# Second mixture: transposing DMAs for the gathered rows and the gate rows, and a fetch of all rows of an expert one expert ahead

## The chip, the cores and the metric

The kernel runs on one core of one Trainium2 chip. The metric is the device time of one execution in microseconds (us). Differences below about 0.2% (4 us) cannot be told from no change.

## What is computed

```python
attn_out = _attn_ref(q, k, v, alpha)                    # gated linear attention: 4 x 8 heads, 768 steps, head size 48
x = attn_out.transpose(0, 2, 1, 3).reshape(B * S, H * D)   # 3072 tokens x 384
x = _moe_ref(x, w_gate, w1, w2)                         # first mixture: all 8 experts on all tokens
# second mixture: the two best of 8 experts for every token
logits = x @ w_gate
noisy_logits = logits + np.log1p(np.exp(x @ w_noise)) * noise
top2 = np.argpartition(-noisy_logits, 2, axis=1)[:, :2]
top2_w = softmax of the two
for e in range(E):
    for k in range(2):
        mask = top2[:, k] == e
        h = np.maximum(x[mask] @ w1[e], 0.0)            # 384 -> 1024
        out[mask] += top2_w[mask, k, None] * (h @ w2[e])   # 1024 -> 384
```

## The kernel before, in words

Attention, the first mixture and the second mixture follow each other on TensorE, and each overlaps the next at its border. Every product is made from float16 high and low parts: three matmuls stand for one.

**Gate rows.** When a tile T of 128 tokens (of 24) is done in the first mixture, `a1` (line 684) makes the high and low float16 halves of its rows, `x` [128, 768], and sends them to DRAM (`xd`, line 688, SP's queue). `a2` (line 691) turns them into columns: six TensorE transposes of 128x128 (line 695) into a PSUM bank, copied to `xf` by ScalarE (line 697). `a3` (line 699) is the gate's matmuls on `xf` (lines 704 and 706). After tile 13 (`G1T` = 14 tiles), and again after tile 23, `route` picks the two best experts of each token and counts ranks.

**Rows of an expert.** An expert has `NJ` = 7 blocks of slots: blocks 0 to 2 (`J0` = 3, 384 slots) and blocks 3 to 6 (448 slots, the last block has 64). `lanes`, `index_rhs` and `index` (lines 802 to 834) make the row numbers of the blocks (a small product, line 815), `gather` (line 839) fetches the 128 rows of a block from `xd` with an indirect DMA of GpSimd's queue into one of eight buffers (`rows`, the room of tiles 0 to 7 of `acc`), and `xpose` (line 847) turns them into columns by six TensorE transposes (line 851) and a ScalarE copy (line 852) into `xh` (even experts) or `xl` (odd experts). In all there are 24 calls of `a2` and 56 of `xpose`.

**Products.** `g1b` (line 854) is the first product of an expert: nine matmuls a unit (line 862), eight units. `g2b` (line 868) is the second: 24 matmuls a block (line 225), a scaling on VectorE (line 874) and an indirect DMA of GpSimd's queue that adds the rows to the output (line 875). The order of stages is (expert 0, blocks 0 to 2), (1, 0 to 2), (0, 3 to 6), (1, 3 to 6), and from expert 2 on both parts of an expert in turn.

**What sets the order.** The program is written in one fixed order. Next to the stream of matmul units a planner's clock runs: after every unit `pump(t)` adds its cost (1.97 for a unit of the first mixture's first product, 0.98 after every pair of `f` steps of a second product, 1.46 for a unit of `g1b` over 384 slots), and `chain` lists of side work have their next item written into the program when the clock has reached its due time; the number beside an item is the time until the next one is due. `need(tag)` pumps without matmuls until a tag is done. `gates` (line 1119) lists a1, a2, a3 for one tile (tiles 0 to 13) or for two (14 to 23), with `GW` = 1.2 after each `a2`. `rows_in` (line 1141) lists lanes, index and gathers, with `GA` = 4.0 after the last gather; `columns` (line 1154) lists the `xpose` calls. `prep` (line 1159) is both. From expert 2 on, at the start of the stage (e, blocks 0 to 2), the chain is `prep(e, J0, NJ)` and then `prep(e + 1, 0, J0)` (line 1242): the late blocks are fetched and turned in the stage before they are used.

**SP's queue.** SP issues the weight loads (lines 111 and 115, two staging buffers `wst`, each load waiting for VectorE's split of the one before the last, line 146), the `xd` stores, and the zeroes written over the output and over `xd` (lines 624 and 628). It works in the program's order, and each entry waits for its own data. GpSimd's queue issues gathers and output additions in the program's order.

Of the kernel before, what the change touches and what calls it, by code (L numbers as in the profile page):

```python
# [10 lines left out]
F16 = mybir.dt.float16  # L11
I32 = mybir.dt.int32
AF = mybir.ActivationFunctionType
# [18 lines left out]

WR = 4.0
GW = 1.2
GA = 4.0
RH = 4.0
SKW = 4.3
# [9 lines left out]
def kernel(ctx, tc, q, k, v, alpha, w_gate, w1a, w2a, g2w, n2w, noise, w1b, w2b, out):  # L47
    nc = tc.nc
    B, NC, _, H, D = v.shape
    E, DM, F = w1a.shape  # L50
    C = 128
    S = NC * C
    NT = B * NC
    NP = H // 2
    KC = DM // 128
# [20 lines left out]
    def bank(shape, dt=F32):  # L76
        return PS["bank"].tile(shape, dt, tag="bank", name="bank")
# [506 lines left out]
    NJ = (H0 + H1 + 127) // 128  # L584
    J0 = H0 // 128
# [4 lines left out]
    G1T = G1  # L590
    BIG = 3.0e38
    OOB = 65536.0
    M2 = {}
# [3 lines left out]
    def m2_setup():  # L597
        sq = ctx.enter_context(tc.tile_pool(name="moe2", bufs=1))
        sr = ctx.enter_context(tc.tile_pool(name="moe2r", bufs=2))
        dr = ctx.enter_context(tc.tile_pool(name="rows", bufs=1, space=bass.MemoryType.DRAM))  # L600
        M2["sr"] = sr
        M2["xd"] = dr.tile([N, 2 * DM], F16, name="xd")

        left_over = [[x, 0] for x in SPARE]

        def t(name, shape, dt=F32):
            n = math.prod(shape[1:]) * (2 if dt == F32 else 1)
            for x in left_over:
                if n >= 384 and x[1] + n <= WT[0].shape[1] - WPL:
                    v = x[0][:, x[1]:x[1] + n]  # L610
                    x[1] += n + n % 2
                    v = v.bitcast(dt) if dt != F16 else v
                    if len(shape) > 2:
                        d = " ".join("abcd"[:len(shape) - 1])
                        v = v.rearrange(f"p ({d}) -> p {d}", **dict(zip("abcd", shape[1:])))
                    M2[name] = v
                    return v
            M2[name] = sq.tile(shape, dt, name=name)
            return M2[name]
# [45 lines left out]
        i16 = t("i16", [128, 128], F16)  # L665
# [16 lines left out]
    XF = {}  # L682

    def a1(T):
        x = M2["sr"].tile([128, 2, DM], F16, name="x16")
        nc.scalar.activation(x[:, 0], acc[:, T, :], AF.Copy, scale=SX2)
        nc.vector.scalar_tensor_tensor(x[:, 1], acc[:, T, :], SX2, x[:, 0], op0=OP.mult, op1=OP.subtract)
        nc.sync.dma_start(M2["xd"][xrow(T):xrow(T) + 128, :], x.rearrange("p a d -> p (a d)"))
        XF[T] = x

    def a2(T):
        x = XF.pop(T)
        p = bank([128, 2 * KC, 128], F16)
        for c in range(2 * KC):
            nc.tensor.transpose(p[:, c, :], x.rearrange("p a (c n) -> p (a c) n", n=128)[:, c, :], M2["i16"])
        XF[T] = M2["sr"].tile([128, 2 * KC, 128], F16, name="xf")
        nc.scalar.activation(XF[T], p, AF.Copy)

    def a3(T):
        x = XF.pop(T)  # L700
        g = M2["g2"]
        p = bank([128, 2, 2 * E])
        for kc in range(KC):
            nc.tensor.matmul(p.rearrange("p a e -> p (a e)"), x[:, kc, :], g[:, kc].rearrange("p a e -> p (a e)"),
                             start=(kc == 0), stop=False, skip_group_check=True)
            nc.tensor.matmul(p[:, 0], x[:, KC + kc, :], g[:, kc, 0], start=False, stop=(kc == KC - 1),
                             skip_group_check=True)
        lo = M2["sr"].tile([128, 2 * E], F32, name="lo")
        nc.scalar.activation(lo, p[:, 1], AF.Copy)
        nc.vector.tensor_add(M2["l2"][:, T, :], p[:, 0], lo)  # L710
# [91 lines left out]
    def lanes(e, T0, T1):  # L802
        for T in range(T0, T1):
            nc.vector.tensor_scalar(M2["lh"][:, T, :], M2["irow"], M2["lane"][:, e, T:T + 1], None, op0=OP.is_equal)

    def index_rhs(e, j0, j1, T1):
        nj = j1 - j0
        nc.vector.tensor_mul(M2["rhs"][:, :T1, j0:j1, :],
                             M2["th"][:, e, :T1, j0:j1, None].to_broadcast([128, T1, nj, 5]),
                             M2["vv"][:, e, :T1, None, :].to_broadcast([128, T1, nj, 5]))  # L810

    def index(e, j0, j1, T1):
        p = bank([128, j1 - j0, 5])
        for T in range(T1):
            nc.tensor.matmul(p, M2["lh"][:, T, :], M2["rhs"][:, T, j0:j1, :], start=(T == 0), stop=(T == T1 - 1))
        slot_rows(p, e, j0, j1)
# [20 lines left out]
    RW = {}  # L837
# [7 lines left out]
        RW[e, j] = r  # L845

    def xpose(e, j, dst):
        r = RW.pop((e, j))
        p = bank([128, 2 * KC, 128], F16)
        for c in range(2 * KC):  # L850
            nc.tensor.transpose(p[:, c, :], r[:, c * 128:(c + 1) * 128], M2["i16"])
        nc.scalar.activation(dst, p[:, :, :dst.shape[2]], AF.Copy)  # L852

    def g1b(x, par, f, xt, n):
        if f == 0:
# [125 lines left out]
    for n, (e, nb) in enumerate(seq):  # L981
        if e == 0 and nb < len(FINE):
            w = FINE[nb]
            a = [[("g1t", 4 * nb + T, w, j) for j in range(FC // 2)] for T in range(0, 4, w)]
# [74 lines left out]
    def chain(items, prio=None):  # L1059
        c = [clk[0], list(items)]  # L1060
        if prio is None:
            chains.append(c)
        else:
            chains.insert(prio, c)
        return c
# [53 lines left out]
    def gates(Ts):  # L1119
        c = []  # L1120
        Ts = list(Ts)
        n = len(Ts)
        for i in range(n + 2):
            if i < n:
                c.append((lambda T=Ts[i]: a1(T), 1.2))
            if 0 <= i - 1 < n:
                c.append((lambda T=Ts[i - 1]: a2(T), GW))
            if i >= 2:
                c.append((lambda T=Ts[i - 2]: a3(T), 0.2, "a3_%d" % Ts[i - 2]))
        return c  # L1130
# [6 lines left out]
    def xt_of(e):  # L1137
        x = xh if e % 2 == 0 else xl
        return x.rearrange("p c n -> p (c n)")[:, :2 * KC * CAP].rearrange("p (c n) -> p c n", n=CAP)

    def rows_in(e, j0, j1, T1, idx_j1):
        c = []
        if idx_j1 is not None:
            for T in range(0, T1, 8):
                c.append((lambda T=T: lanes(e, T, min(T + 8, T1)), 1.0))
            c.append((lambda: index_rhs(e, j0, idx_j1, T1), RH))
            c.append((lambda: index(e, j0, idx_j1, T1), 1.5, "i%d" % e))
        else:
            c.append("i%d" % e)
        for j in range(j0, j1):  # L1150
            c.append((lambda j=j: gather(e, j), 0.0 if j < j1 - 1 else GA))
        return c

    def columns(e, j0, j1):
        xt = xt_of(e)
        return [(lambda j=j: xpose(e, j, xt[:, :, j * 128:min(j * 128 + 128, CAP)]), 0.8, "x%d_%d" % (e, j))
                for j in range(j0, j1)]

    def prep(e, j0, j1, T1, idx_j1):
        return rows_in(e, j0, j1, T1, idx_j1) + columns(e, j0, j1)  # L1160
# [11 lines left out]
    while gi < len(stream):  # L1172
# [12 lines left out]
        elif g[0] in ("g1", "s1"):  # L1185
            e, nb, f = g[1:]
# [14 lines left out]
        else:  # L1201
            e, nb, j = g[1:]
# [5 lines left out]
            if e == E - 1:  # L1208
                T = 4 * nb + j
                if T < G1T:  # L1210
                    c = gates([T])
# [10 lines left out]
    w_queue(E + 1)  # L1222
    r = route(G1T, NT)
    chain(["a3_%d" % (NT - 1)] + r[:-1] + [r[-1] + ("r2",)] + ["x1_%d" % (J0 - 1)]
          + prep(0, J0, NJ, NT, NJ) + prep(1, J0, NJ, NT, NJ) + prep(2, 0, J0, NT, NJ))

    def u1(m, f):
        e, j0, j1 = order2[m]
        n = min(CAP, j1 * 128)
        g1b(E + e, m % 2, f, xt_of(e)[:, :, j0 * 128:n], n - j0 * 128)  # L1230
# [5 lines left out]
    for m in range(len(order2) + 1):  # L1236
        a, c = [], []
        if m < len(order2):
            e, j0, j1 = order2[m]
            a = [(lambda f=f: u1(m, f), 9 * ((min(CAP, j1 * 128) - j0 * 128) / 2400.0 + 0.0025)) for f in range(FC)]  # L1240
            if m >= 4 and j0 == 0:
                chain(prep(e, J0, NJ, NT, None) + (prep(e + 1, 0, J0, NT, NJ) if e + 1 < E else []))
        if m:
            e, j0, j1 = order2[m - 1]
            c = [(lambda j=j: u2(m - 1, j), 0.98) for j in range(j0, j1)]
            if j1 == NJ and e + 2 < E:
                def fin(f=c[-1][0], x=E + e + 2):
                    f()
                    w_queue(x)
                c[-1] = (fin, 0.98)  # L1250
        if m <= 4:
            units = c + a
        else:
            units, i = [], 0
            for k_, x in enumerate(a):
                units.append(x)
                while i < len(c) and (i + 1) * len(a) <= (k_ + 1) * len(c):
                    units.append(c[i])
                    i += 1
            units += c[i:]  # L1260
        for u, t in units:
            if a and u is a[0][0]:
                need("x%d_%d" % (order2[m][0], order2[m][2] - 1))
                w_need(E + order2[m][0])
            u()
            pump(t)
# [42 lines left out]
```

## Time and profile before

| | us |
|---|---|
| median of 3 runs | 2095.74 (2094.11 to 2097.69) |
| profiled execution, its own time | 2102.97 |
| its span, first to last instruction | 2101.2 |
| TensorE busy in the span | 2016.1 |
| VectorE, ScalarE, GpSimd busy | 1229.3, 725.8, 625.4 |
| mean granted TensorE clock | 0.990 of full |

A profile has one row for a group of instructions: the source line, the engine, the operation, the tile that it writes and those that it reads, how many there are, their busy time and the mean of one. A timeline row gives the start, the length in us, and in brackets how long the engine stood idle before it and what ended the wait. Matmuls are pipelined: the spacing of starts, not the length of one, is what a matmul costs. The second mixture's own stages run from about 1613 us to the end; the gate rows are turned between 1440 and 1625 us.

### The profile page before, as it was taken

To read this page: it belongs to the slowest core of one execution; us is meant where nothing else is said; L and a number is where in the kernel's file an instruction comes from. 1 tells how busy PE (TensorE), PEld (TensorE's weight loads), DVE (VectorE), ACT (ScalarE), POOL (GpSimd) and SP (SyncE) were. 2 spreads that over 40 slices of the span, in tenths; PEclk is the share of its full clock that TensorE was granted. 3 is DMA by queue.
4 is the path that set the end of the run, shared out by engine and by line. 5 is a ranking of instruction groups with operands and counts; after the bars stand their busy time and mean duration, and the time that the engine had idled before them with its cause. 6 is when DMAs were issued, how large, how long until landed. Compare 5 with 4: busy or idle time off the path is not lost. (4 is left out here: it accounts for less than half of the span.)

```text
span 2101.2 us, 38370 instructions
## 1 busy us (share of the span) xinstructions
PE 2016.1 (96%) x16123; PEld 1361.2 (65%) x16123; DVE 1229.3 (59%) x2513; ACT 725.8 (35%) x1277; POOL 625.4 (30%) x452
## 2 busy tenths in 40 slices
PE   6999999999999999999999999999999999999996
PEld 5887656667766766677667766775556565555553
DVE  8889574765675585566557556554345655444431
ACT  5554422432342243333333333223334233333230
POOL 2433212522442253234324332230001243323322
PEclk9999999999999999999999999999999999999998
DMA  6333010100010020010001001004112334433331
GB/s 212 96 105 105 21 41 21 47 16 1 26 36 1 1 61 2 1 34 29 1 11 51 1 1 41 1 2 152 57 42 84 84 91 121 96 73 87 84 76 23
DMA packets 61855, 106.94 MB, mean 51 GB/s; under 512 B 10980, under 2 KB 44029, under 8 KB 61680
## 3 DMA queue, kind: packets, MB, share of 16 engines
q1 hardware_dynamic: 50256, 85.05, 12.7%
q0 software_dynamic: 11136, 18.89, 5.2%
q8 instruction: 127, 2.08, 0.4%
q10 hardware_dynamic: 288, 0.52, 0.1%
q14 instruction: 48, 0.39, 0.1%
HBM read 85.17 MB, written 21.63 MB: 51 GB/s over the span
## 5 line engine op out<-in xcount | busy, mean ns | idle before, releaser
L272 PE MATMUL bank<-xh,wt 128*128 128x512 f16 x1728 | 521.9, 380 | 6.2 <-DVE ss L295 3.8
L306 PE MATMUL long<-wt,hid 128*128 128x192 f16 x6048 | 508.8, 246 | 14.1 <-DVE acc L316 9.2
L291 POOL TENSOR_TENSOR hid<-ss,hid 128x1024 f16<-128x1024 f32 x144 | 307.1, 2132 | 706.1 <-ACT hid L290 651.7
L306 PEld LDWEIGHTS <-hid 128*128 128x128 f16 x6048 | 499.6, 98 | 27.0 <-issue 11.1
L272 PEld LDWEIGHTS <-wt 128*128 128x128 f16 x2592 | 253.1, 98 | 306.2 <-PE bank L272 6.1
L225 PE MATMUL bank<-wt,hid 128*128 128x384 f16 (+1 forms) x2496 | 430.5, 328 | 1.8 <-DVE hid L866 1.8
L225 PEld LDWEIGHTS <-hid 128*128 128x128 f16 (+1 forms) x2496 | 242.2, 99 | 156.6 <-issue 5.2
L272 PE MATMUL bank<-xl,wt 128*128 128x512 f16 x864 | 328.2, 380 | 0.0
L316 DVE SCALAR_TENSOR_TENSOR acc<-long,Pm,acc 128x192 f32<-128x192 f32 (+1 forms) x360 | 187.3, 533 | 169.8 <-PE long L306 167.5
L295 DVE SCALAR_TENSOR_TENSOR ss<-bank,ss 128x256 f32<-128x256 f32 x576 | 241.5, 421 | 58.3 <-ACT hid L284 39.6
L295 DVE SCALAR_TENSOR_TENSOR hid<-bank,hid 128x256 f16<-128x256 f32 (+1 forms) x288 | 158.9, 552 | 180.9 <-ACT ss L279 180.9
L290 ACT ACTIVATE hid<-ss 128x1024 f16<-128x1024 f32 x144 | 152.2, 1057 | 241.2 <-DVE ss L295 241.2
L146 DVE SCALAR_TENSOR_TENSOR wt<-wst,wt 128x1024 f16<-128x1024 f32 (+3 forms) x129 | 167.2, 1308 | 36.9 <-ACT wt L144 36.1
L278 ACT ACTIVATE hid<-bank 128x256 f16<-128x256 f32 x144 | 53.4, 371 | 382.4 <-PE bank L272 382.4
L875 POOL DMA_INDIRECT out_dram<-acc,ix x56 | 91.5, 1634 | 296.5 <-DVE acc L874 245.6
L862 PEld LDWEIGHTS <-wt 128*128 128x128 f16 x1152 | 110.9, 98 | 86.4 <-issue 4.7
L866 DVE SCALAR_TENSOR_TENSOR hid<-bank,hid 128x384 f16<-128x384 f32 (+1 forms) x128 | 74.9, 589 | 109.5 <-ACT hid L865 109.3
L865 ACT ACTIVATE hid<-bank 128x384 f16<-128x384 f32 (+1 forms) x128 | 65.8, 517 | 205.1 <-PE bank L862 201.6
L144 ACT ACTIVATE wt<-wst 128x1024 f16<-128x1024 f32 (+3 forms) x129 | 111.4, 883 | 70.9 <-DMA wst<-in_moe_w_dram 47.3
L194 PE MATMUL bank<-xh,wt 128*128 128x512 f16 x384 | 120.0, 379 | 0.7 <-DVE acc L316 0.7
L862 PE MATMUL bank<-xh,wt 128*128 128x384 f16 (+1 forms) x576 | 109.1, 343 | 0.9 <-ACT xh L852 0.9
L284 ACT ACTIVATE hid<-bank 128x512 f16<-128x512 f32 x144 | 86.0, 597 | 66.4 <-PE bank L272 66.4
(188 smaller groups left out, 1792.7 us busy)
## 6 DMA issues: line engine op xcount, KB each, us to landing
wst<-in_moe_w_dram SPq DMA_DIRECT2D x45, 512.0 KB, 3.3
wst<-in_moe_w_dram SPq DMA_DIRECT2D x60, 384.0 KB, 3.2
la<-in_alpha_dram SPq DMA_DIRECT2D x24, 260.0 KB, 2.7
lk<-in_k_dram SPq DMA_DIRECT2D x24, 256.0 KB, 3.0
wt<-in_q_dram SPq DMA_DIRECT2D x22, 256.0 KB, 3.9
out_dram<-zero SPq DMA_DIRECT2D x6, 768.0 KB, 4.4
xd<-x SPq DMA_DIRECT2D x24, 192.0 KB, 1.9
wt<-in_v_dram SPq DMA_DIRECT2D x16, 192.0 KB, 4.1
```

The lines of the kernel that those rows point to most:

```text
L144: nc.scalar.activation(t[:, o:o + n], src, AF.Copy, scale=SW)
L146: nc.vector.scalar_tensor_tensor(t[:, o + o1:o + o1 + n], src, SW, t[:, o:o + n], op0=OP.mult, op1=OP.subtract)
L194: nc.tensor.matmul(p, w1s(e, a, kc, f), x[:, kc, s], start=(n == 0), stop=(n == 3 * KC - 1))
L225: nc.tensor.matmul(p, h(a, f, s), w2s(x, b, f), start=(f + n == 0), stop=(f == FC - 1 and n == 2))
L272: nc.tensor.matmul(p, w1s(e, a, kc, f), x[:, kc, tok], start=(n == 0), stop=(n == 3 * KC - 1))
L290: nc.scalar.activation(lefts(e, nb, j, 0, S1, 4), sums, AF.Copy)
L291: nc.gpsimd.tensor_sub(lefts(e, nb, j, 1, S1, 4), sums, lefts(e, nb, j, 0, S1, 4))
L295: nc.vector.scalar_tensor_tensor(out, p, 0.0, x, op0=OP.max, op1=op)
L306: nc.tensor.matmul(out, left(e, nb, j, a, aop)[:, q * 128:(q + 1) * 128], w2t(e, b, wop, j), start=start and n == 0, stop=stop and n == 3 ...
L316: nc.vector.scalar_tensor_tensor(a, p, Pm[:, T, e:e + 1], a, op0=OP.mult, op1=OP.add)
L862: nc.tensor.matmul(p, w1s(x, a, kc, f), xt[:, b * KC + kc, :], start=(i == 0), stop=(i == 3 * KC - 1))
L875: nc.gpsimd.indirect_dma_start(out=out, out_offset=bass.IndirectOffsetOnAxis(ap=ix, axis=0), in_=y, in_offset=None, bounds_check=N - 1, oo ...
```

## The change

`a2` and `xpose` call one function, `turn`. For tile 13 and for blocks 0 to 2 of expert 0 it does what was done before; everywhere else one transposing DMA on SP's queue takes the rows from SBUF and writes the columns to SBUF, with no TensorE and no ScalarE instruction. `xf` gets a pool of three buffers of its own. After the last `a2` of a chain the planner waits 4.0 (`GT`) in place of 1.2, except for tile 13. From expert 2 on all seven blocks of an expert are fetched one expert ahead: `rows_in(e + 1, 0, NJ)`, followed by `columns` for blocks 0 to 2 in the same stage; blocks 3 to 6 are turned in the stage before they are used.

```diff
+GT = 4.0
...
+        M2["st"] = ctx.enter_context(tc.tile_pool(name="moe2t", bufs=3))
...
+    def turn(dst, src, on_pe):
+
+        if not on_pe:
+            nc.sync.dma_start_transpose(out=dst, in_=src[:dst.shape[2]])
+            return
+        p = bank([128, 2 * KC, 128], F16)
+        for c in range(2 * KC):
+            nc.tensor.transpose(p[:, c, :], src[:, c * 128:(c + 1) * 128], M2["i16"])
+        nc.scalar.activation(dst, p[:, :, :dst.shape[2]], AF.Copy)
+
     def a2(T):
         x = XF.pop(T)
-        p = bank([128, 2 * KC, 128], F16)
-        for c in range(2 * KC):
-            nc.tensor.transpose(p[:, c, :], x.rearrange("p a (c n) -> p (a c) n", n=128)[:, c, :], M2["i16"])
-        XF[T] = M2["sr"].tile([128, 2 * KC, 128], F16, name="xf")
-        nc.scalar.activation(XF[T], p, AF.Copy)
+        XF[T] = M2["st"].tile([128, 2 * KC, 128], F16, name="xf")
+        turn(XF[T], x.rearrange("p a d -> p (a d)"), T == G1T - 1)
...
     def xpose(e, j, dst):
-        r = RW.pop((e, j))
-        p = bank([128, 2 * KC, 128], F16)
-        for c in range(2 * KC):
-            nc.tensor.transpose(p[:, c, :], r[:, c * 128:(c + 1) * 128], M2["i16"])
-        nc.scalar.activation(dst, p[:, :, :dst.shape[2]], AF.Copy)
+        turn(dst, RW.pop((e, j)), e == 0 and j < J0)
...
-                c.append((lambda T=Ts[i - 1]: a2(T), GW))
+                c.append((lambda T=Ts[i - 1]: a2(T), GT if i == n and Ts[-1] != G1T - 1 else GW))
...
     chain(["a3_%d" % (NT - 1)] + r[:-1] + [r[-1] + ("r2",)] + ["x1_%d" % (J0 - 1)]
-          + prep(0, J0, NJ, NT, NJ) + prep(1, J0, NJ, NT, NJ) + prep(2, 0, J0, NT, NJ))
+          + prep(0, J0, NJ, NT, NJ) + prep(1, J0, NJ, NT, NJ) + rows_in(2, 0, NJ, NT, NJ) + columns(2, 0, J0))
...
             if m >= 4 and j0 == 0:
-                chain(prep(e, J0, NJ, NT, None) + (prep(e + 1, 0, J0, NT, NJ) if e + 1 < E else []))
+                chain(columns(e, J0, NJ) + (rows_in(e + 1, 0, NJ, NT, NJ) + columns(e + 1, 0, J0) if e + 1 < E else []))
```

## Rows read from the trace of the kernel before

**Rows 1.** Page, part 1: busy us (share of the span) xinstructions of each engine
```profile
PE 2016.1 (96%) x16123; PEld 1361.2 (65%) x16123; DVE 1229.3 (59%) x2513; ACT 725.8 (35%) x1277; POOL 625.4 (30%) x452
```

**Rows 2.** Waits of PE from 1400 us on: in total, times, longest
```profile
PE bank L851 <- DMA acc<-xd,ix: 10.1, 5, 2.8
```

**Rows 3.** Groups by line and form: the transposes
```profile
L851 PE MATMUL bank<-i,acc 128*128 128x128 f16 x336 | 28.6, 223 | 10.2 <-DMA acc<-xd,ix 10.1
...
L695 PE MATMUL bank<-i,x 128*128 128x128 f16 x144 | 12.1, 219 | 1.1 <-DVE x L687 1.0
```

**Rows 4.** Timeline of PE: one gate tile, from its `a2` to the next
```profile
1466.26 0.50 PE L695 MATMUL bank<-i,x 128*128 128x128 f16 x6
1466.59 2.11 PE L225 MATMUL bank<-wt,hid 128*128 128x384 f16 x12
...
1470.64 0.38 PE L194 MATMUL bank<-xh,wt 128*128 128x512 f16 x1
...
1474.53 0.50 PE L695 MATMUL bank<-i,x 128*128 128x128 f16 x6
```

**Rows 5.** Timeline of PE: one `xpose` inside an expert's stage
```profile
1925.62 0.50 PE L851 MATMUL bank<-i,acc 128*128 128x128 f16 x6
1925.96 1.87 PE L862 MATMUL bank<-xl,wt 128*128 128x448 f16 x9
```

**Rows 6.** Timeline of PE: the longest wait for a gather
```profile
1834.17 3.09 PE L225 MATMUL bank<-wt,hid 128*128 128x384 f16 x18
1840.08 0.58 PE L851 MATMUL bank<-i,acc 128*128 128x128 f16 x6 [2.83 <-DMA acc<-xd,ix]
```

**Rows 7.** Windows: busy of PE, PEld, DVE, ACT, POOL, then PEclk, DMA share, GB/s
```profile
1800.00:1850.00 50.00, 47.17 (x295) 27.83 (x294) 20.95 (x47) 17.60 (x27) 15.92 (x12) 0.97 0.44 107
...
1950.00:2000.00 50.00, 47.61 (x321) 28.51 (x320) 20.75 (x55) 15.24 (x26) 17.31 (x13) 0.97 0.35 83
```

**Rows 8.** DMA issues: queue, count, KB each, median us to landing
```profile
xd<-x SPq DMA_DIRECT2D x24, 192.0 KB, 1.9
...
acc<-xd,ix POOLq DMA_INDIRECT x56, 3.1
...
wg<-in_moe_w_gate_dram SPq DMA_DIRECT2D x1, 12.0 KB, 6.8
```

**Rows 9.** Timeline of PE: last pair of gate tiles and late blocks of expert 0
```profile
1613.26 1.63 PE L862 MATMUL bank<-xh,wt 128*128 128x384 f16 x9
...
1618.29 0.50 PE L695 MATMUL bank<-i,x 128*128 128x128 f16 x6
...
1620.42 0.50 PE L695 MATMUL bank<-i,x 128*128 128x128 f16 x6
...
1622.55 0.18 PE L704 MATMUL bank<-g,xf 128*128 128x32 f16 x1
...
1671.90 12.08 PE L862 MATMUL bank<-xh,wt 128*128 128x448 f16 x63 [0.94 <-ACT xh L852]
```

**Rows 10.** Timeline of POOL: gathers of expert 0's late blocks
```profile
1661.58 1.55 POOL L875 DMA_INDIRECT out_dram<-acc,ix  x1 [10.28 <-DVE acc L874]
1663.44 1.08 POOL L842 DMA_INDIRECT acc<-xd,ix  x1 [0.31 <-issue]
...
1667.48 1.00 POOL L842 DMA_INDIRECT acc<-xd,ix  x1 [0.30 <-issue]
```

**Rows 11.** Timeline of SP: the store of the gate tile of rows 4
```profile
1466.33 0.33 SPq L688 DMA_DIRECT2D xd<-x  x1
```

**Rows 12.** Waits of SP's queue, 1640 to 2060 us: in total, times, longest
```profile
SPq L111 <- DVE wt L146: 279.1, 18, 69.9
SPq L115 <- DVE wt L146: 57.4, 23, 4.0
```

**Rows 13.** Timeline of ACT: expert 1's last weight splits
```profile
1641.85 0.84 ACT L144 ACTIVATE wt<-wst 128x768 f16<-128x768 f32 x1 [4.48 <-DMA wst<-in_moe_w_dram]
```

## The prediction

> **What bounds the kernel now.** I read the page's busy times first: TensorE is busy 96% of the span, VectorE 59%, ScalarE 35%, GpSimd 30% [rows 1]. So a TensorE instruction that goes is worth its full time, and one that another engine loses is worth nothing unless TensorE waits for it. Second, the waits of TensorE from 1400 us on: the one large entry is transposes of line 851 waiting for the gather that fetched their rows, 10.1 us in five waits [rows 2]. Third, the groups by line: 336 and 144 transposes, 28.6 and 12.1 us busy [rows 3], which are 80 sets of six. Fourth, the timeline, for what one set costs in the stream: the second product resumes 0.33 us after the set of a gate tile starts [rows 4], the first product 0.34 us after that of a gathered block [rows 5].
>
> **The change part by part.** *Transposes off TensorE.* Of 24 `a2`, 23 leave TensorE; of 56 `xpose`, 53 do. That is 76 sets x 0.336 us = **-25.5 us**. It is certain as far as TensorE's own time goes. The ScalarE copies go too, and I cost that at nothing: ScalarE is idle 65% of the time, and what TensorE waits for is not there.
>
> *Waits for gathers.* From expert 2 on, the late blocks' rows are there one stage or more before they are turned, and TensorE no longer reads them but the columns, which are written at the start of the stage before the one that needs them. In a stage of some 27 us four transfers have to end; even at the slowest price below they take 4 x 6.8 = 27 us. So the five waits go: **-10.1 us**. [...] What is late next there: nothing I find, the gathers' own row buffers are freed by transfers written into the program at least 10 us ahead.
>
> *What a transposing DMA takes.* No row shows one. Bounds by the nearest rows: 1.9 us from issue to landing, for the store of the same 192 KB by the same queue, and 6.8 us, for 12 KB that are moved in pieces of a few elements [rows 8]. I take 3.1 us, the gather of the same 192 KB, since it too handles the 128 rows apart. Below I call it X.
>
> *The gate tiles, 0 to 12.* `a3` was due 1.2 after `a2`, and is due 4.0 after it now. By the units that follow (24 matmuls of the second product, 3.9 us, then one unit of the first product, half of 1470.64 to 1474.53 = 1.94 us) [rows 4] it comes 5.8 us after the place of `a2`. The transfer is issued behind the store of the tile, at 1466.33 + 0.33 [rows 11], about 0.4 us after that place, so it may take 5.4 us. At 3.1 nothing waits. The zeroes of the next tile now stand behind the transfer in SP's queue, and cover nothing. For the five pairs of tiles 14 to 23, two transfers in a row have about 7 us from the first issue (2.1 us between the two [rows 9], 4.0, and one pump); 6.2 fits. A weight load that waits ahead of a transfer in SP's queue (line 115) waited up to 4.0 us [rows 12]; for one or two tiles this can show. **+1 us**, between 0 and 6.
>
> *The late blocks of expert 0.* Here the cover is thin: the chain from tile 23's gate through `route`, index and gather to the columns ends at the first product at 1671.90, which already waited for it [rows 9]. (i) `a3` of the last pair came one `g1b` unit (1.63 us, clock 1.46) after its last `a2` [rows 9], and 4.0 needs three: two units, 3.3 us later. (ii) The last gather is issued at 1667.48 and lands 3.1 us later [rows 8, 10]; turned 3.1 us after that is 1673.7, where it was 1671.9: 1.8 us. (iii) 3.3 us later in the program, the four gathers fall behind one more output addition in GpSimd's queue, 1.6 us [rows 10]. Together 6.7 us; the four sets x 0.336 = 1.3 us that I counted as saved are no gain here, since TensorE waits. **+8 us**, between 0 (the chain finds VectorE less loaded) and 14 (the addition itself has to wait for the one before it, and the clock falls).
>
> *Weights.* The transfers stand in SP's queue between the weight loads, and each load waits for VectorE (279.1 us in 18 waits, [rows 12]) only because SP runs ahead of the program; what is written behind a load is not due before it. The loads that ran far ahead now come behind the transfers, yet still before their splits. Only expert 1's are tight: ScalarE already waits 4.48 us for one of them [rows 13], and five transfers are put ahead of some of its loads. **+1 us**, between 0 and 4. GpSimd's queue now has seven gathers in a row instead of four and three; each is 1.0 us of issue, and the additions behind them have four buffers: nothing.
>
> **Sum:** -25.5 - 10.1 - 3.0 + 1 + 8 + 1 = -28.6 us, 2102.97 to 2074.4 for the profiled execution. That execution was 7.2 us above the median of the runs shown; against 2095.74 it gives **2067**.
>
> [...] The rows bound one transfer between 1.9 and 6.8 us [rows 8]. [...]
>
> **Rivals.** *First, everything hides.* If the hand-over to expert 0's late blocks costs nothing and no gate waits: -38.6 us, 2057. For: VectorE is what paces `route`, and a later start may be absorbed there. Against: that product already waited. *Second, SP's queue and the hand-over cost twice what I take:* +14, +4 and +6 against -38.6 is -15 us, 2081. For: several entries of one queue, each waiting for its own data, in the one region where loads, stores and turns are all due. Against: SP is idle most of the time.
>
> *Third, slower: the transposing transfer is long, and transfers follow each other singly,* so that the gate's matmuls (line 704) wait for `xf`. Single tiles wait X - 5.4 each (13 of them), pairs 2X - 7 each (5), and the four late blocks of expert 0 end 4X - 7 later than their gathers allow beyond what I took. At X = 6.8: 18 + 33 + 20 = 71 us, so -28.6 + 71 = +42, **2138**. It decides from X of about 5.2 (0 + 17 + 14 = 31 us, all the gain). For: no row excludes it, and one 12 KB transfer of small pieces does take 6.8 us. Against: both 192 KB transfers between the same places take 1.9 and 3.1. *Fourth, the change does not do what it says:* the fetch ahead brings nothing since a row buffer is freed too late, and the hand-over eats most of the rest: within 4 us of before.
>
> **How the numbers follow.** Forecast 0.58 (own range 2058 to 2076), everything hides 0.14, the second rival 0.13, slower 0.12, no change 0.03. A measurement of this kernel can tell about 0.2%, 4 us, from no change. Faster by more than that is 0.58 + 0.14 + 0.13 = 0.85, within it 0.03, slower 0.12. The range reaches from just under the first rival, 2055, to beyond the second, 2088; the slow rival, the fourth and some edge, under 0.2, stay outside.
>
> **What would show it.** Right: lines 695 and 851 with 6 and 18 transposes left; no wait of line 851 for a gather after 1700 us; transposing DMAs on SP's queue that land in 2 to 4 us; matmuls of line 704 that follow without a wait; a longer pause than 0.94 us before expert 0's late blocks. From expert 2 on, each expert's period should be some 4 to 5 us shorter (seven sets of 0.336 and one wait of 2 us). Wrong: line 704 waiting for `xf` on a DMA tile after tile (third rival), or line 862 waiting for `xh` or `xl` at every stage, or SP held by each transfer for longer than 3 us.

## The result, and the profile after

| | before | after |
|---|---|---|
| median of the runs, us | 2096.51 (4 runs, 2094.11 to 2097.69) | 2074.62 (4 runs, 2071.85 to 2077.93) |
| profiled execution, its own time, us | 2102.97 | 2075.67 |
| its span, us | 2101.2 | 2073.9 |

The ratio is 0.9891, 95% interval 0.987 to 0.9911: 21.9 us off the median. Run again beside other versions, the same kernel gave 0.9881 (0.9862 to 0.9900). The forecast was 28.6 us off, 2067 us, with a range of 2055 to 2088.

The page's busy times after, where [rows 1] stands for before:

```profile
PE 1984.0 (96%) x15667; PEld 1332.4 (64%) x15667; DVE 1228.6 (59%) x2513; ACT 671.5 (32%) x1201; POOL 622.2 (30%) x452
```

TensorE has 456 matmuls fewer, which are 76 sets of six, and 32.1 us less of busy time; ScalarE has 76 copies less, of which TensorE had waited for one (0.94 us at 1671.90, [rows 9]). The waits of TensorE from 1380 us on (what waited, for whom: us in total, times, longest), against [rows 2]:

```profile
PE bank L867 <- DMA xh<-acc: 12.4, 1, 12.4
PE bank L713 <- DMA xf<-x: 4.0, 2, 2.4
PE bank L824 <- DVE rhs L817: 2.2, 1, 2.2
PE bank L226 <- DVE hid L871: 1.3, 2, 1.1
PE bank L195 <- DVE acc L317: 0.7, 1, 0.7
```

The five waits for gathers are gone. In their place stand one long wait, for the columns of expert 0's late blocks, and a small new one, the gate (now line 713) for `xf`. A wait of an index (line 815, now 824) for VectorE was there before too, and has moved: from expert 0's late blocks (1657.92 us) to expert 3 (1733.66 us). Before it was

```profile
PE bank L815 <- DVE rhs L808: 2.0, 1, 2.0
```

Cutting both spans at the same instructions shows where the time went. The starts are from the two timelines (1439.85, 1549.03, 1613.26, 1671.90, 1754.37 and 2062.40 us before; 1437.34, 1543.03, 1604.65, 1668.72, 1751.07 and 2034.02 after); the sets are those that left TensorE in that stretch:

| stretch, up to | before, us | after, us | difference | sets off, x 0.336 us |
|---|---|---|---|---|
| store of tile 0's rows | 1439.85 | 1437.34 | -2.5 | 0 |
| store of tile 13's rows | 109.18 | 105.69 | -3.5 | 13: 4.4 |
| first product of expert 0, blocks 0 to 2 | 64.23 | 61.62 | -2.6 | 8: 2.7 |
| first product of expert 0, late blocks | 58.64 | 64.07 | +5.4 | 9: 3.0 |
| second product of expert 2, late blocks | 82.47 | 82.35 | -0.1 | 14: 4.7 |
| last five blocks of expert 7 | 308.03 | 282.95 | -25.1 | 32: 10.8 |
| end | 38.80 | 39.88 | +1.1 | 0 |

The first line is not the change's: nothing differs there but the execution. The view by windows (length; busy of PE, PEld, DVE, ACT, POOL; granted clock, DMA share, GB/s) has a lower clock in the first 100 us of the execution of before, whose row comes first:

```profile
0.00:100.00 100.00, 79.04 (x1009) 67.65 (x1010) 85.75 (x132) 49.65 (x93) 30.33 (x39) 0.95 0.48 161
```

```profile
0.00:100.00 100.00, 78.59 (x1050) 66.89 (x1051) 88.60 (x136) 51.55 (x98) 30.80 (x39) 1.00 0.49 162
```

So the two spans differ by 2.5 us before the change acts: tile 0's store starts at 1439.85 us in the execution with 0.95 and at 1437.34 in the one with 1.00.

The stretch of experts 3 to 7 gives 25.1 us, more than its sets, since the waits for gathers were there too. The two stretches around expert 0's late blocks lost 23 sets, 7.7 us, and got longer by 5.3 us together. The hand-over, in the timelines of PE, of DVE and of POOL (start, length, instruction, idle before it):

```profile
1650.64 0.76 PE L824 MATMUL bank<-rhs,acc 128*128 128x20 bf16 x24
1651.25 5.04 PE L226 MATMUL bank<-wt,hid 128*128 128x384 f16 x30
1668.72 14.62 PE L867 MATMUL bank<-xh,wt 128*128 128x448 f16 x63 [12.43 <-DMA xh<-acc]
```

```profile
1651.93 0.16 DVE L838 SCALAR_TENSOR_TENSOR ix<-sf 128x4 int32<-128x4 f32 x1
```

```profile
1650.15 1.56 POOL L880 DMA_INDIRECT out_dram<-acc,ix  x1 [11.07 <-DVE acc L879]
1655.56 1.56 POOL L880 DMA_INDIRECT out_dram<-acc,ix  x1 [3.84 <-issue]
1657.42 1.08 POOL L851 DMA_INDIRECT acc<-xd,ix  x1 [0.30 <-issue]
...
1661.46 0.99 POOL L851 DMA_INDIRECT acc<-xd,ix  x1 [0.30 <-issue]
```

Here is a thing to see: the row numbers were ready at 1652.1 us, and GpSimd did nothing for 3.84 us, and yet the first gather started at 1657.42. It stood behind the output addition of 1655.56 in GpSimd's queue. What that addition waited for the profile does not name here (`issue`); for four other additions of this execution, 15.7 us of idle GpSimd in all, it names the landing of an earlier one, and so for one in experiment 1:

```profile
1660.58 1.56 POOL L882 DMA_INDIRECT out_dram<-acc,ix  x1 [4.20 <-DMA out_dram<-acc,ix]
```

What a turn takes, in the list of DMA issues (queue, operation, count, median us from issue to landing), which [rows 8] could only bound:

```profile
xl<-acc SPq DMA_TRANSPOSE x28, 4.1
xh<-acc SPq DMA_TRANSPOSE x25, 4.0
xf<-x SPq DMA_TRANSPOSE x23, 2.8
```

and on SP's queue, around one gate tile (compare [rows 11]):

```profile
1463.67 0.33 SPq L690 DMA_DIRECT2D xd<-x  x1
1464.10 2.28 SPq L696 DMA_TRANSPOSE xf<-x  x1
1466.43 0.57 SPq L626 DMA_DIRECT2D out_dram<-zero  x1
1471.61 0.33 SPq L690 DMA_DIRECT2D xd<-x  x1
1472.03 1.21 SPq L696 DMA_TRANSPOSE xf<-x  x1
```

The stores here hold the queue for 0.33 us, the turns for 1.21 and 2.28.

### The profile page after: what moved, and what is told of

Same layout as the page of the kernel before. It is cut to its first block, busy times and chain, and to the rows that moved or that the text cites. A ratio compares the mean times of both kernels' runs of the same rounds, so it can differ in the third digit from the quotient of the medians.

```text
span 2073.9 us, 37502 instructions
## 1 busy us (share of the span) xinstructions
PE 1984.0 (96%) x15667; PEld 1332.4 (64%) x15667; DVE 1228.6 (59%) x2513; ACT 671.5 (32%) x1201; POOL 622.2 (30%) x452
## 5 line engine op out<-in xcount | busy, mean ns | idle before, releaser
L226 PE MATMUL bank<-wt,hid 128*128 128x384 f16 (+1 forms) x2496 | 422.4, 326 | 1.3 <-DVE hid L871 1.3
L867 PE MATMUL bank<-xh,wt 128*128 128x384 f16 (+1 forms) x576 | 107.6, 345 | 12.4 <-DMA xh<-acc 12.4
```

Of the source, the lines that this page charges most:

```text
L226: nc.tensor.matmul(p, h(a, f, s), w2s(x, b, f), start=(f + n == 0), stop=(f == FC - 1 and n == 2))
L867: nc.tensor.matmul(p, w1s(x, a, kc, f), xt[:, b * KC + kc, :], start=(i == 0), stop=(i == 3 * KC - 1))
```

## The experiments

The theory behind all: a set of transposes on TensorE costs its time in the stream (0.336 us), a turn by DMA costs nothing where its columns are not due before they land, and what was given back came from places without that cover, above all the hand-over to expert 0's late blocks, where the order in GpSimd's queue holds the gathers back. The rivals: SP's queue or the transfers themselves are what is late; or only the removed waits for gathers were worth anything.

**Experiment 1, the gathers ahead of the second addition.**

```diff
+RH0 = 4.0
+GI0 = 0.0
...
-    def rows_in(e, j0, j1, T1, idx_j1):
+    def rows_in(e, j0, j1, T1, idx_j1, rh=RH, gi=1.5):
...
-            c.append((lambda: index_rhs(e, j0, idx_j1, T1), RH))
-            c.append((lambda: index(e, j0, idx_j1, T1), 1.5, "i%d" % e))
+            c.append((lambda: index_rhs(e, j0, idx_j1, T1), rh))
+            c.append((lambda: index(e, j0, idx_j1, T1), gi, "i%d" % e))
...
-          + prep(0, J0, NJ, NT, NJ) + prep(1, J0, NJ, NT, NJ) + rows_in(2, 0, NJ, NT, NJ) + columns(2, 0, J0))
+          + rows_in(0, J0, NJ, NT, NJ, RH0, GI0) + columns(0, J0, NJ) + prep(1, J0, NJ, NT, NJ) + rows_in(2, 0, NJ, NT, NJ) + columns(2, 0, J0))
```

> The changed kernel, with the wait between index and gather of expert 0's late blocks cut from 1.5 to 0 on the planner's clock, so that the four gathers stand before the second of expert 1's output additions in GpSimd's queue and not behind it. Theory (queue order): the row numbers were ready at 1652.1 us, the first gather started at 1657.42 behind that addition, which waited for the one before it; so the gathers start some 5 us earlier, the wait of line 867 for xh falls from 12.4 to 6 to 8 us, and the time from 2074.6 to 2068 to 2070 us. Rival (SP's queue or the transposing transfers themselves hold the columns back): the wait stays at 11 to 13 us and the time within 1 us of 2074.6.

Measured: ratio 0.9865 (0.9849 to 0.9881), median 2070.62 us. The wait and the queue, in the waits of PE and the timeline of POOL:

```profile
PE bank L869 <- DMA xh<-acc: 7.6, 1, 7.6
```

```profile
1646.57 1.56 POOL L882 DMA_INDIRECT out_dram<-acc,ix  x1 [11.07 <-DVE acc L881]
1649.42 1.08 POOL L853 DMA_INDIRECT acc<-xd,ix  x1 [1.29 <-DVE wc L843]
```

The gather now follows one addition instead of two and waits for its row numbers alone. The wait fell by 4.8 us, and from the first product of expert 0 to that of its late blocks it is 58.69 us (1660.28 - 1601.59), against 64.07 in the changed kernel. The two intervals of the time overlap, so the time alone does not separate it from the changed kernel; the wait does, and it is the place that the queue theory names.

**Experiment 2, expert 0's late blocks by TensorE.**

```diff
-        turn(dst, RW.pop((e, j)), e == 0 and j < J0)
+        turn(dst, RW.pop((e, j)), e == 0)
```

> The changed kernel, with expert 0's late blocks turned by TensorE and ScalarE as before (four transfers less). Theory (queue order): only the last leg gets shorter, 3.8 us of landing of the last transfer against 0.34 + 0.81 us; the wait before line 867's first product of these blocks, now for the gather, stays at 8 to 11 us, and the time falls by 1 to 3 us. Rival (SP's queue or the transfers hold the columns back): the wait falls under 3 us and the time by 9 us or more.

Measured: ratio 0.9866 (0.9850 to 0.9883), median 2072.59 us. Waits of PE:

```profile
PE bank L700 <- DMA acc<-xd,ix: 5.2, 3, 4.5
PE bank L867 <- ACT xh L701: 0.6, 1, 0.6
```

Between the two theories: the waits are 5.8 us in sum, less than the 8 to 11 expected and more than the rival's 3, probably because TensorE turns the first blocks (from 1662.44 us) while the last is still coming (its gather is issued at 1663.03). The time does not separate this kernel from the changed one (the intervals overlap). Counted from the first product of expert 0, the late blocks' product starts after 60.4 us (1666.87 - 1606.51), against 64.07 in the changed kernel and 58.64 before. So the transfers' landing is worth 3.7 us there, net of the four sets that are back on TensorE, more than the 2.7 (3.8 - 0.34 - 0.81) of the expectation. What remains goes with the gathers' late start: they still begin 5.2 us after their row numbers. Neither theory is the whole.

**Experiment 3, the gate rows' part alone** (line 696's DMA for `a2`; `xpose` and the fetch as before the change).

```diff
-        turn(dst, RW.pop((e, j)), e == 0 and j < J0)
+        turn(dst, RW.pop((e, j)), True)
...
-          + prep(0, J0, NJ, NT, NJ) + prep(1, J0, NJ, NT, NJ) + rows_in(2, 0, NJ, NT, NJ) + columns(2, 0, J0))
+          + prep(0, J0, NJ, NT, NJ) + prep(1, J0, NJ, NT, NJ) + prep(2, 0, J0, NT, NJ))
...
-                chain(columns(e, J0, NJ) + (rows_in(e + 1, 0, NJ, NT, NJ) + columns(e + 1, 0, J0) if e + 1 < E else []))
+                chain(prep(e, J0, NJ, NT, None) + (prep(e + 1, 0, J0, NT, NJ) if e + 1 < E else []))
```

> The gate rows' part of the change alone: a2 by transposing DMA with its 4.0, gathered rows by TensorE and fetched as before the change. Theory (TensorE's time is what is bought): 23 sets of 0.336 us are 7.7 us off, 4 us come back as waits of line 713 for xf and 1 to 3 us by the later route, so 2096.5 becomes 2089 to 2095 us. Rival (the whole gain is the removed wait for gathers, transposes were free): 2096 to 2101 us, since only waits are added.

Measured: ratio 0.9990 (0.9981 to 1.0000), 2098.24 beside 2099.83 us before: 1.6 us of the 7.7 that 23 sets are. That is the very edge of the theory's 1.5 to 7.5 us and within what can't be told from no change, which the rival has; the time does not decide between them. Waits of PE:

```profile
PE bank L700 <- DMA acc<-xd,ix: 15.5, 9, 4.8
PE bank L713 <- DMA xf<-x: 2.7, 1, 2.7
```

The gate's own wait is 2.7 us, on tile 0. Of the 15.5 us for gathers, 10.1 are the old ones (the waits after 1690 us sum to that); 5.4 are new and stand at the hand-over. Here no gathered row is turned by DMA, so this part of the hand-over's price comes with the later gate of the last pair; in this kernel's timeline too the four gathers follow a second addition (1657.83 us, after 3.95 us of idle GpSimd). With the gate's wait, that is what ate the sets.

**Experiment 4, the gathered rows' part alone** (`a2` by TensorE with its 1.2).

```diff
-        turn(XF[T], x.rearrange("p a d -> p (a d)"), T == G1T - 1)
+        turn(XF[T], x.rearrange("p a d -> p (a d)"), True)
...
-                c.append((lambda T=Ts[i - 1]: a2(T), GT if i == n and Ts[-1] != G1T - 1 else GW))
+                c.append((lambda T=Ts[i - 1]: a2(T), GW))
```

> The gathered rows' part alone: xpose by transposing DMA with the fetch one expert ahead, a2 by TensorE as before with its 1.2. Theory: 53 sets of 0.336 us are 17.8 us off, the five waits for gathers and their slow clock 13 to 14 us, and the hand-over to expert 0's late blocks gives 5 to 8 us back: 2070 to 2074 us. Rival (the whole gain is the removed wait): 2086 to 2090 us.

Measured: ratio 0.9893 (0.9877 to 0.9910), 2077.96 beside 2099.83 us: 21.9 us, the whole gain of the change. As a ratio that is the upper edge of what the theory said (2074 of 2096.5 us is 0.9893), and far from the rival. The wait for expert 0's late columns is 5.4 us here, not 12.4: the gate is not later, and the gathers begin 4.0 us after their row numbers (1662.03 against 1658.0), as before the change.

**Experiment 5, the fetch ahead alone** (experiment 4's edit, and line 857 with `True`: all sets on TensorE).

> Only the fetch one expert ahead; every set of transposes stays on TensorE and a2 keeps its 1.2. Theory (two separate gains in the experts' stages): the five waits for gathers and the slow clock after them go, 13 to 14 us, and nothing else moves: ratio 0.993 to 0.9945 to the kernel before. The rest of what the gathered rows' part alone gave (ratio 0.9893) is then TensorE's time for 53 sets. Rival (the wait only moves: TensorE waits elsewhere when the transposes still stand in its stream): ratio 0.998 to 1.001.

Measured: ratio 0.9962 (0.9949 to 0.9975), 2089.41 beside 2098.13 us. This lies between the two expectations and meets neither. The fetch alone is 8.7 us by the medians; the rest of the gathered rows' 21.9, some 13 us, is TensorE's time for the sets, less what the hand-over costs in experiment 4. Two things make the fetch look smaller here than in the changed kernel. New waits for gathers stand before expert 3, 1.8 us in sum. And the sets stand in other places than before the change: an expert takes 56.5 us from index to index (1846.46 - 1790.00), against 53.4 in the changed kernel (1841.30 - 1787.85) and 58.5 to 60.5 before, so its seven sets are worth 3.0 us, 0.43 each. Three of them stand among the matmuls of the expert's last block, whose weights are 64 columns, and there a set costs more than 0.336 us: those 24 matmuls take 5.70 us with three sets in between, and 4.02 in the changed kernel, 0.56 a set.

```profile
1798.62 0.51 PE L700 MATMUL bank<-i,acc 128*128 128x128 f16 x6
1799.06 1.16 PE L226 MATMUL bank<-wt,hid 128*64 128x384 f16 x6
```

**Experiment 6, turns doubled** where the theory says that they are hidden.

```diff
-        turn(dst, RW.pop((e, j)), e == 0 and j < J0)
+        r = RW.pop((e, j))
+        turn(dst, r, e == 0 and j < J0)
+        if 3 <= e < E:
+            d2 = M2["st"].tile([128, 2 * KC, 128], F16, name="xf")
+            turn(d2[:, :, :dst.shape[2]], r, False)
```

> The changed kernel, with each of the 35 turns of experts 3 to 7 done a second time into a buffer that nobody reads. Theory (hidden there): SP is held 1.25 us more and the DMA engines some 1.2 us more per turn, under work that is not due; ratio 0.988 to 0.991, as the changed kernel's 0.9891. Rival (SP's queue or the DMA engines are near their limit in these stages): weight loads and additions come late, 35 x 0.3 us or more, ratio 0.994 or above.

Measured: ratio 0.9893 (0.9878 to 0.9908). The stretch of experts 3 to 7, cut at the same two instructions, in the view by windows (length; busy of PE, PEld, DVE, ACT, POOL; granted clock, DMA share, GB/s), first of the changed kernel, then of this one:

```profile
1751.07:2034.02 282.95, 282.95 (x1750) 164.79 (x1749) 127.98 (x283) 70.59 (x117) 88.35 (x68) 1.00 0.57 114
```

```profile
1749.56:2032.51 282.95, 282.95 (x1751) 164.78 (x1749) 127.96 (x283) 71.35 (x117) 87.81 (x67) 1.00 0.66 135
```

Thirty-five more transfers, the DMA engines busier by 0.09, and not 0.01 us of difference. There a turn is free.

**Experiment 7, the 4.0 taken back** (`GW` after every `a2`, turns as in the changed kernel).

```diff
-                c.append((lambda T=Ts[i - 1]: a2(T), GT if i == n and Ts[-1] != G1T - 1 else GW))
+                c.append((lambda T=Ts[i - 1]: a2(T), GW))
```

> The changed kernel with 1.2 in place of 4.0 after the last a2. Theory (lead against landing): a3 then comes 1.95 us after a2's place and the columns land 3.2 to 3.4 us after it, so line 713 waits 1.3 us or so on each of tiles 1 to 12 and 2 to 5 us on tile 0: 15 to 20 us of waits for xf in all; the hand-over gains 1 to 4 us; ratio 0.995 to 0.998. Rival (the 4.0 only delays route and is not needed): waits for xf under 5 us, ratio 0.988 or below.

Measured: ratio 1.0038 (1.0027 to 1.0050): slower than before the change. Waits of PE, and its timeline at tiles 0 and 2:

```profile
PE bank L713 <- DMA xf<-x: 27.8, 15, 5.4
...
PE bank L867 <- DMA xh<-acc: 5.6, 1, 5.6
```

```profile
1443.16 0.21 PE L713 MATMUL bank<-g,xf 128*128 128x32 f16 x1 [5.35 <-DMA xf<-x]
...
1443.34 4.00 PE L226 MATMUL bank<-wt,hid 128*128 128x384 f16 x12
...
1468.84 0.19 PE L713 MATMUL bank<-g,xf 128*128 128x32 f16 x1 [1.15 <-DMA xf<-x]
...
1469.01 2.11 PE L226 MATMUL bank<-wt,hid 128*128 128x384 f16 x12
```

The direction was as the theory has it and the size was beyond it. Tiles 2 and 3 wait 1.15 and 1.20 us, near what was worked out (1.3). But the longest wait cost twice: after its 5.35 us, twelve matmuls took 4.00 us where they take 2.11 after the 1.15 us of tile 2, and the mean granted clock from 1436 to 1545 us is 0.95 here and 1.00 in the changed kernel.

**Experiment 8, turns by DMA only where they are covered.** From experiment 1's version, with

```diff
-        turn(XF[T], x.rearrange("p a d -> p (a d)"), T == G1T - 1)
+        turn(XF[T], x.rearrange("p a d -> p (a d)"), T == 0 or T >= G1T - 1)
...
-        turn(dst, RW.pop((e, j)), e == 0 and j < J0)
+        turn(dst, RW.pop((e, j)), e == 0)
...
-                c.append((lambda T=Ts[i - 1]: a2(T), GT if i == n and Ts[-1] != G1T - 1 else GW))
+                c.append((lambda T=Ts[i - 1]: a2(T), GT if i == n and 0 < Ts[-1] < G1T - 1 else GW))
```

> Transposing DMAs only where the cover is thick: gate tiles 1 to 12, and the gathered rows from expert 1 on; tiles 0 and 13 to 23 (with 1.2) and all blocks of expert 0 by TensorE; the gathers of expert 0's late blocks without the 1.5 after index. Theory: 12 + 49 sets of 0.336 us are 20.5 us off, 13 to 14 us of waits go, and the hand-over costs 2 to 5 us more than before, with waits of 4 to 7 us there; ratio 0.9850 to 0.9875. Rival (the gate rows' part is worth nothing wherever it is used, since what TensorE saves there it waits later): ratio 0.988 to 0.990.

Measured: ratio 0.9842 (0.9828 to 0.9855), 2065.76 beside 2098.13 us, better than expected, and its interval lies below the changed kernel's. No wait for a DMA is left on TensorE after 1380 us:

```profile
PE bank L826 <- DVE rhs L819: 4.1, 2, 2.2
PE bank L228 <- DVE hid L873: 2.0, 2, 1.1
PE bank L197 <- DVE acc L319: 0.7, 1, 0.7
```

**Experiments 9 and 10, the change once more and experiment 8 with all gate tiles on TensorE** (`True` in its `a2`, `GW` after every `a2`), on one chip.

> The changed kernel once more, beside the two versions below and on their chip. Both theories: ratio 0.987 to 0.991 to the kernel before.

Measured: 0.9881 (0.9862 to 0.9900), with the same wait of 12.4 us.

> The version that turned out fastest (transposing DMAs for gate tiles 1 to 12 and for the gathered rows from expert 1 on), with all gate tiles on TensorE. Theory (a turn that is covered is worth its 0.336 us): the 12 sets are 4.0 us, so this is 3 to 5 us slower than that version, ratio 0.9855 to 0.9870. Rival (gate turns by DMA are worth nothing): ratio 0.9835 to 0.9850, as that version.

Measured: 0.9857 (0.9838 to 0.9876), where experiment 8, on another chip, had 0.9842. The difference, 0.0015 or 3.1 us, is near the 4.0 of twelve sets and in the theory's band; the intervals overlap, so this is a leaning, no proof.

**Experiment 11, the index of expert 3 later.** The wait of 2.2 us for `rhs` that came with the change. In the changed kernel, SP's queue, then ScalarE and TensorE:

```profile
1718.52 0.38 SPq L116 DMA_DIRECT2D wst<-in_moe_w_dram  x1
1718.99 5.56 SPq L696 DMA_TRANSPOSE xh<-acc  x4
1724.64 1.06 SPq L116 DMA_DIRECT2D wst<-in_moe_w_dram  x1
1725.75 2.57 SPq L696 DMA_TRANSPOSE xh<-acc  x2
```

```profile
1729.53 0.84 ACT L145 ACTIVATE wt<-wst 128x768 f16<-128x768 f32 x1 [5.42 <-DMA wst<-in_moe_w_dram]
```

```profile
1733.66 0.76 PE L824 MATMUL bank<-rhs,acc 128*128 128x35 bf16 x24 [2.24 <-DVE rhs L817]
```

Four turns stand between two weight loads; ScalarE waits 5.42 us for the load, VectorE's share of the split (1730.40 us) waits 3.48 us for ScalarE, `rhs` (1732.58 us) comes behind it in VectorE's order, and TensorE waits 2.24 us for `rhs`. In the kernel before, ScalarE's longest wait for a load from 1690 to 1740 us is 2.31 us, and no wait stands at this index, nor in experiment 5, which fetches as early but has no turn in SP's queue. Experiment 5's row for it:

```profile
1731.28 0.77 PE L824 MATMUL bank<-rhs,acc 128*128 128x35 bf16 x24
```

```diff
-                chain(columns(e, J0, NJ) + (rows_in(e + 1, 0, NJ, NT, NJ) + columns(e + 1, 0, J0) if e + 1 < E else []))
+                chain(columns(e, J0, NJ) + (rows_in(e + 1, 0, NJ, NT, NJ, 8.0 if e == 2 else RH) + columns(e + 1, 0, J0) if e + 1 < E else []))
```

`rh` is the parameter that experiment 1 added to `rows_in`. The edit does not move the loads; it lets TensorE come later.

> The fastest version, with 8.0 in place of 4.0 between rhs and index of expert 3, so that TensorE does not come to that index before VectorE has made rhs; VectorE is late there because ScalarE waits for weight loads that stand behind turns in SP's queue. Theory (the turns' price on the weight loads shows as this one wait): the wait of 2.2 us for rhs at 1726 us goes, and with the slow clock after it 2 to 4 us: ratio 0.9825 to 0.9835. Rival (the wait only moves to the next reader of the late weights): waits from 1700 to 1780 us stay at 2 us or more in sum, ratio 0.984 or above.

Measured: ratio 0.9826 (0.9808 to 0.9843), 2065.45 beside 2102.64 us. Between 1690 and 1790 us TensorE has no wait left; of those for `rhs` only the one at expert 0's late blocks, which the kernel before had too, stays (2.0 us). This is the fastest version, 1.7% under the kernel before; against experiment 8 the time itself is unclear, the vanished wait is plain.

## Why the prediction was right, point by point

The direction, the mechanism and the range held. The forecast for the runs was 2067 and the median 2074.62, so 21.9 us were gained and not 28.6. The profiled execution fell from 2102.97 to 2075.67, where the sum said 2074.4; that it came so close is in part luck. Of its 27.3 us, 2.5 lie before tile 0's store, where the clock of the first 100 us differed and the kernels do not, and 1.1 come back at the end. Between them, where the change acts, it gained 25.9 us: what was given back was larger than the sum had it, by 2.9 at the hand-over and 1.1 at the weights, and the waits for gathers gave 1.2 us more. The rest of the miss is the last step, which moved the profile's sum to the median of the runs: the profiled execution of before was 6.5 us above its runs' median, that of after 1.05. The slow start of the one can explain some 2.5 us of that difference; the rest stays open.

*Transposes off TensorE, -25.5 us.* All 76 sets went, and 0.336 us holds at the places where they stood: before the change an expert took 58.54 us from one index to the next (1859.19 to 1917.73) with one wait of 2.57, and after it 53.45, which leaves 2.5 us for seven sets. The 0.43 of experiment 5 belongs to that kernel's places. That ScalarE's copies cost nothing was wrong for one of them, the 0.94 us of [rows 9], which lies in the hand-over.

*Waits for gathers, -13.1 us with the clock.* By the two profiles the stretch of experts 3 to 7 lost 25.1 us. Sets are 10.8 of it and the waits 10.1; the other 4.2 are mostly slow matmuls behind two of the waits, as here in the kernel before, at a granted clock of 0.50 from 1960 to 1963 us, nine that take 1.63 us at 1.00:

```profile
1960.71 2.89 PE L862 MATMUL bank<-xh,wt 128*128 128x384 f16 x9
```

The 3.0 us that the sum has for the slow clock were the author's estimate, and no run shows that term by itself; what the two profiles showed in its place is this 4.2.

By runs, the fetch alone gave 8.7 us (ratio 0.9949 to 0.9975, 5.2 to 10.7 us). With the 2.7 us that the sets of experts 3 to 7 cost more in experiment 5's places (296.36 - 282.95 us, less 10.8) and its 1.8 us of new waits, that is an estimate of 13 us, so the two agree. An expert's period shrank by 5.1 to 7.0 us where 4 to 5 were named. The waits were no chance of one execution: experiment 3, which fetches as before the change, has 10.1 us of them after 1690 us.

*A turn takes 3.1 us.* Measured: 2.8 for gate rows, 4.0 to 4.1 for gathered rows. The bounds of 1.9 and 6.8 held for these medians; the slowest single turn took 9.8. The third rival, whole transfers of more than 5.2 us one after another, did not come: the four before expert 0's late blocks hold SP for 5.68 us in all and land 3.1 to 4.8 us after issue. The 2.8 us of a gate tile's turn stand against 1.9 us for the store of the same bytes.

*Gate tiles, +1 us.* The wait for `xf` was 4.0 us, inside the bound of 6: 2.42 on tile 0, whose turn stood behind a weight load that was itself issued only at 1440.30, three us after the tile's store, and 1.59 on the last pair, whose turns stand between those of expert 1. Experiment 7 shows that the lead was read rightly: with it, tiles 1 to 12 wait for nothing; without it tiles 2 and 3 wait 1.15 and 1.20 us, tile 1 waits 3.83, and all tiles together 27.8 where it was 4.0. The gate rows' part as a whole was worth little to the change (1.6 us alone in experiment 3; experiment 4 has the whole gain without it): the tiles bought what the hand-over gave back.

*Late blocks of expert 0, +8 us.* Up to the product the sum was right: the stretch grew by 5.4 us where nine sets were 3.0, which makes 8.4. (i) I gave the later gate 3.3 us; from the first product of expert 0 to the index it was 1.3 more (45.99 against 44.66 us), with five sets, 1.7 us, gone there: 3.0. (ii) The last leg, from the last gather's issue to the product, grew from 4.4 to 7.3 us, 2.9 and not 1.8, besides the four sets: gather and turn take 7.3 us together, and not 3.1 each. (iii) From row numbers to the first gather there were 4.0 us before ([rows 10] and VectorE's rows) and 5.3 after, 1.3 and not 1.6. What I did not price is what the wait does afterwards: the mean granted clock from 1668.72 to 1683.18 us is 0.82 (0.50 from 1670 to 1672 us, 1.00 from 1674 us on), and 63 matmuls took 14.62 us where [rows 9] has 12.08. With this 2.5 us the hand-over cost 10.9 and not 8.

*Weights, +1 us.* I looked for it at expert 1, and it stood at expert 3: 2.24 us (experiment 11). The sentence that failed is that the loads still come before their splits; behind four turns stood one for which ScalarE waited 5.42 us.

The first rival (all hidden) was excluded by the 12.4 us. The second (SP's queue and the hand-over at twice the price), 15 us off, lies 6.4 us from the median, a little nearer than the forecast (7.6), and 12 from the profile. Its places were the right ones; its prices, 14 + 4 + 6 us, were not: hand-over, weights and gate took 10.9, 2.1 and 0.9 in the profile.

## What to carry to other kernels

In this kernel a transpose that TensorE does between matmuls was worth moving to a DMA only where the columns were due later than the transfer landed, counted from the issue and with every transfer ahead of it in that queue; where a product waited for them, the same transfer cost more than it saved. Look for the consumer in each stage and choose per stage, not per operation. A gather that was written behind an accumulating transfer stood until that transfer could start, 3.84 us of idle GpSimd; written ahead of it, it took 4.8 us off TensorE's wait.

## What the runs showed of the hardware

The turns, of up to 128 rows of 1.5 KB, were moved in many small packets: the page counts 57,725 packets more for 14.1 MB and 76 turns, some 760 each, of 245 bytes on average. In the changed kernel a turn of gate rows held SP's queue for 1.21 to 2.28 us, at its least nearly four times a store's 0.33. Six transposes between other matmuls cost 0.336 us in the stream, 56 ns each, though one lasts 219 ns in [rows 3]; that is why so little was to be gained per set. And a wait's price was not its length: experiment 7 had 23.8 us more of waits for `xf` than the changed kernel and 6.8 less at the hand-over, and it was 31 us slower (0.0147 of 2098 us), with the mean granted clock at 0.95 over the tiles that waited.
